# Two steps share one network of 512 tokens in float32r, with weights streamed from DRAM

## The chip, the cores and the metric

One core of one Trainium2 chip runs the kernel. The metric is device microseconds per execution. The engines are TensorE (PE, with its weight loads as PEld), VectorE (DVE), ScalarE (ACT), GpSimd (POOL) and SyncE (SP), which issues DMAs.

## The reference

A gated linear attention over 768 positions feeds a two-layer network with a PReLU between the layers.

```python
# q, k, v, f_logit: (4, 8, 768, 48);  w_in (384, 2048), w_out (2048, 384), alpha (2048,)
f = 1 / (1 + exp(-f_logit))
for t in range(768):
    state = f[:, :, t, :, None] * state + einsum('bhd,bhe->bhde', k[:, :, t], v[:, :, t])
    y[:, :, t] = einsum('bhd,bhde->bhe', q[:, :, t], state)
x = y.transpose(0, 2, 1, 3).reshape(3072, 384)
h = x @ w_in
out = (maximum(h, 0) + alpha * minimum(h, 0)) @ w_out
```

## The kernel before

The 3072 tokens are cut into 12 steps: step n = (c, bp) has 128 positions (C) of two batches (U), that is T = 256 tokens; c goes from 0 to 5, bp is 0 or 1, and n = 2c + bp. Each step has an attention part and a network part, and the network of step n runs beside the attention of step n+1.

The order of work on PE, DVE and ACT is written out by hand. Every part is a generator that is advanced piece by piece, and `ORDER` lists which generator comes next. The letters in it: `P` (prepare, six pieces), `O` (carry, one), `S` (attend, six), `n` (network, 13 pieces, or 12 for the first step), `a w b v` (the unpacking of the weights), `W` (sums of blocks of w_out). Steps 0 and 1 have a finer alphabet. The DMAs on SP and POOL are not in that list; they wait for what they need, in the order in which their queue has them. From step 4 on the order repeats (`USUAL`): "S n2 S n2 O n Q n3 Q S2 n Q S n Q S n Q n Q n", where Q is the prepare part of the step after.

The pieces that the prediction's steps speak of:
- `prepare` piece 1 calls `loaded` (lines 264 to 297): POOL loads f, q, k and v of the step (L272, L281), ACT takes the sigmoid (L283), and DVE makes running products of f. Piece 2 is two scans. Piece 3 (L336, L342) is the last to read f. Pieces 4 and 5 scale keys and queries; piece 5 transposes scaled keys on DVE into `kt` (L413). Piece 6 copies queries into A on ACT (L380) and issues sixteen small DMAs on SP from `kt` to `ksn` (L422). Each of f, q, k, us, ps and ksn has one buffer; y uses that of ksn.
- `carry` multiplies `ksn` by v (L436), takes the cross terms (L463) and moves the state (`moved`, L447 and L451, on DVE).
- `attend` has two pieces of scores (L489, L498) with masked copies on DVE (L506, L553), two pieces that place the blocks on ACT (L513), one that multiplies by v (L521), and one that moves the state, copies y and sends it by ten DMAs on three queues to xT (`by_token`, L533).
- `network`: eight pieces of the first layer, each for two feature tiles of 128 in one PSUM bank (12 records in the trace), then ACT (L721) and DVE (L723) make the gate, and after every fourth piece DVE makes four sums (L800). The second layer is a Strassen-Winograd form of seven products of eight matmuls of 192 columns (L755) with five `plus` on DVE (L759). Step 0 has the plain second layer instead (L736, 32 matmuls of 384 columns).

```python
kt = late["kt"].tile([128, W], F32, tag="kt", name=f"kt_{i}")
```

In the kernel before this tile has a buffer of its own. PSUM has four banks for the network (`bank`) and two pairs of banks for attention (`pair`).

Of the kernel before, what the change touches and what calls it, by code (L numbers as in the profile page):

```python
# [8 lines left out]
F32 = mybir.dt.float32  # L9
I16 = mybir.dt.int16  # L10
# [4 lines left out]
AF = mybir.ActivationFunctionType  # L15
# [6 lines left out]
U = 2  # L22
# [6 lines left out]
UP = 2.0 ** 16  # L29

# [5 lines left out]
        "n0 1u1 1u0 n0 1U0 b v 1U1 P2 1H0 1A0 v 1d n0 1H1 b 1t 1D v 1y0 1A1 1y1 v W 1Y0 P2 1Y1 W 1X W W n0 1M P2 P2 "  # L36
        "P2 n0 n1 S2 P2 W n1 n1 n1 n1 ",
        "S2 S2 P3 n1 P3 n1 n1 O2 P3 S2 n1 n1 S2 P3 P3 n1 S2 n1 n1 S3 n2 P3 n2 S3 n2 n2 P4 n2 S3 S3 n2 O3 n2 n2 S3 S3 "
        "P4 n2 P4 n2 P4 P4 n2 P4 n2 n2 ",
)  # L40
USUAL = "S n2 S n2 O n Q n3 Q S2 n Q S n Q S n Q n Q n"

def flat(head, usual, steps=12):
    out = []
    for word in " ".join(head).split():
        if word in "awbvW":
            out.append((word, None))
        elif word[0] in "01":
            out.append((word[1:], int(word[0])))
        else:  # L50
            out.append((word[0], int(word[1:])))
    for n in range(len(head), steps + 1):
        for key in usual.split():
            for _ in range(int(key[1:] or 1)):
                k = key[0]
                m = n - 1 if k == "n" else n + 1 if k == "Q" else n
                if 0 <= m < steps:
                    out.append(("P" if k == "Q" else k, m))
    return out

ORDER = flat(HEAD, USUAL)
# [3 lines left out]
def kernel(  # L65
# [57 lines left out]
    staging = ExitStack()  # L123
    stage = staging.enter_context(tc.tile_pool(name="stage", bufs=1))
# [10 lines left out]
    w_in_sb = const.tile([128, NK, DF], F32, tag="w_in", name="w_in_sb")  # L135
    w_out_sb = const.tile([128, NF, DM], F32, tag="w_out", name="w_out_sb")
    NH, DH = NF // 2, DM // 2
    gate = const.tile([128, NH, 2, T], F32, tag="gate", name="gate")
# [244 lines left out]
    def prepare(bp, c, x):  # L383
# [28 lines left out]
        kt = late["kt"].tile([128, W], F32, tag="kt", name=f"kt_{i}")  # L412
# [125 lines left out]
    def attend(bp, c, x):  # L538
# [32 lines left out]
        xT = x["T"] = work.tile([128, NK, T], F32, tag="xT", name=f"xT_{i}")  # L571
# [3 lines left out]
    def opening(bp, x):  # L575
# [110 lines left out]
        def given():  # L686
            xT = x["T"] = work.tile([128, NK, T], F32, tag="xT", name=f"xT_{i}")
            if bp:
                by_token(x["y"], xT)
            else:  # L690
                for kt in range(NK):
                    nc.scalar.copy(xT[:, kt], x["xt"][kt][:, 0:T])
# [13 lines left out]

    def network(bp, c, x):
        i = f"{bp}_{c}"
        xT = x["T"]
        plain = (bp, c) == steps[0]  # L710
        for f in range(NH):
            ph = bank(f"ph{f}_{i}")
            tiles = (2 * f, 2 * f + 1) if plain else (f, f + NH)
            for kt in range(NK):
                for j, m in enumerate(tiles):
                    nc.tensor.matmul(ph[:, j * T:(j + 1) * T], lhsT=w_in_sb[:, kt, m * 128:(m + 1) * 128],  # L716
                                     rhs=xT[:, kt], start=(kt == 0 and j == 0), stop=(kt == NK - 1 and j == 1),
                                     skip_group_check=True)
            neg = work.tile([128, 2, T], F32, tag="neg", name=f"neg{f}_{i}")
            phv = ph.rearrange("p (j t) -> p j t", j=2)  # L720
            nc.scalar.activation(neg, phv, AF.Relu, scale=-1.0)  # L721
            for j, m in enumerate(tiles):
                nc.vector.scalar_tensor_tensor(gate[:, m % NH, m // NH], neg[:, j], om[:, m:m + 1], phv[:, j],  # L723
                                               ALU.mult, ALU.add)
            if not plain and f % 4 == 3:
                sums(slice(f - 3, f + 1))
            yield

        def store(u, o):
            t0 = ((U * bp + u) * NC + c) * C  # L730
            nc.sync.dma_start(out=out[t0:t0 + C], in_=o)

        if plain:
            po = [bank(f"po{u}_{i}") for u in range(U)]
            for n, (f, u) in enumerate([(f, u) for f in range(NF) for u in range(U)]):
                nc.tensor.matmul(po[u][:, 0:DM], lhsT=gate[:, f % NH, f // NH, u * C:(u + 1) * C], rhs=w_out_sb[:, f],  # L736
                                 start=(f == 0), stop=(f == NF - 1))
                if n % 8 == 7 and n != U * NF - 1:
                    yield
            for u in range(U):  # L740
                o = work.tile([128, DM], F32, tag="o", name=f"o{u}_{i}")
                nc.scalar.activation(o, po[u][:, 0:DM], AF.Copy, scale=UP)
                store(u, o)
            yield
            return

        a11, a12, a22 = (lambda f, j=j, u=u: gate[:, f, j, u * C:(u + 1) * C] for j, u in ((0, 0), (1, 0), (1, 1)))
        s1, s2, s3, s4 = (lambda f, n=n: late["S"][:, n, f] for n in range(4))
        b11, t1, b21, b22 = (lambda f, r=r, d=d: w_out_sb[:, NH * r + f, DH * d:DH * (d + 1)]
                             for r, d in ((0, 0), (0, 1), (1, 0), (1, 1)))  # L750
        t2, t3, t4 = (lambda f, t=t: late[t][:, f] for t in ("t2", "t3", "t4"))

        def product(to, of, by, more=False):
            for f in range(NH):
                nc.tensor.matmul(to[:, 0:DH], lhsT=of(f), rhs=by(f), start=(f == 0 and not more), stop=(f == NH - 1),  # L755
                                 skip_group_check=True)

        def plus(to, of, by, scale=UP):
            nc.vector.scalar_tensor_tensor(to, of[:, 0:DH], scale, by, ALU.mult, ALU.add)  # L759

        o0, o1 = (work.tile([128, DM], F32, tag="o", name=f"o{u}_{i}") for u in range(U))
        kept, u2, u3 = (late["C"][:, n] for n in range(3))
        pa, pb = (bank(f"p{n}_{i}") for n in "ab")
        product(pa, a11, b11)
        product(pb, a22, t4)
        nc.scalar.activation(kept, pa[:, 0:DH], AF.Copy, scale=UP)
        yield
        pc, pd = (bank(f"p{n}_{i}") for n in "cd")
        product(pc, s2, t2)
        product(pd, s1, t1)  # L770
        plus(u2, pc, kept)
        yield
        product(pa, a12, b21, more=True)
        product(pc, s3, t3, more=True)
        plus(o0[:, DH:DM], pd, u2)
        nc.scalar.activation(o0[:, 0:DH], pa[:, 0:DH], AF.Copy, scale=UP)  # L776
        yield
        pe = bank(f"pe_{i}")
        product(pe, s4, b22)
        plus(u3, pc, kept)  # L780
        plus(o1[:, 0:DH], pb, u3, -UP)
        plus(o1[:, DH:DM], pd, u3)
        store(1, o1)
        yield
        plus(o0[:, DH:DM], pe, o0[:, DH:DM])
        store(0, o0)
        yield

    late = {}

    def sums(fs_):

        s = late["S"]
        u0, u1 = slice(0, C), slice(C, T)
        of = lambda j, u: gate[:, fs_, j, u]
        for to, x_, y_, op in ((s[:, 0, fs_], of(0, u1), of(1, u1), ALU.add),
                               (s[:, 1, fs_], s[:, 0, fs_], of(0, u0), ALU.subtract),
                               (s[:, 2, fs_], of(0, u0), of(0, u1), ALU.subtract),
                               (s[:, 3, fs_], of(1, u0), s[:, 1, fs_], ALU.subtract)):
            nc.vector.tensor_tensor(to, x_, y_, op)  # L800

    def halves_of_w_out():

        staging.close()
        pool = ctx.enter_context(tc.tile_pool(name="late", bufs=1))
        late["kt"] = pool
        late["S"] = pool.tile([128, 4, NH, C], F32, tag="S", name="S")
        late["C"] = pool.tile([128, 3, DH], F32, tag="C", name="Csum")
        for n in ("t2", "t3", "t4"):
            late[n] = pool.tile([128, NH, DH], F32, tag=n, name=n)  # L810
        yield
        b11, b12, b21, b22 = (w_out_sb[:, NH * r:NH * (r + 1), DH * d:DH * (d + 1)] for r in range(2) for d in range(2))
        t2, t3, t4 = (late[n] for n in ("t2", "t3", "t4"))

        for to, x_, y_, op in ((t3, b22, b12, ALU.subtract), (t2, t3, b11, ALU.add), (t4, t2, b21, ALU.subtract),
                               (b12, b12, b11, ALU.subtract)):
# [3 lines left out]
            yield  # L820
# [8 lines left out]
    pieces["W"] = halves_of_w_out()  # L829

    with tc.manual_schedule(engines={mybir.EngineType.PE, mybir.EngineType.DVE, mybir.EngineType.Activation}):
# [3 lines left out]
        for n, (bp, c) in enumerate(steps):  # L835
            x = {}
            run["n", n] = network(bp, c, x)
# [6 lines left out]
        for key, n in ORDER:  # L844
            part = pieces[key] if n is None else run[key, n]
            part() if callable(part) else next(part)

# [54 lines left out]
```

## Time and profile before

| | |
|---|---|
| time, median of 3 runs (lowest to highest) | 606.79 us (604.29 to 607.48) |
| span of the profiled execution, first to last instruction | 604.5 us |
| DVE busy | 495.7 us (82%) |
| ACT busy | 249.5 us (41%) |
| granted TensorE clock | 1.00 throughout |
| DMA moved | 50.41 MB, 83 GB/s on average |
| length of a step from step 3 on | 46.7 to 48.9 us |

The profile is of one execution; no time of its own is given beside its span, and the three runs are other executions. Shares of busy time are averages over the whole span; the stretches in the table of busy time show one step each.

### The profile page before, as it was taken

How to read it: one execution, taken by the hardware profiler on the slowest of the kernel's cores; microseconds unless marked ns; L12 is line 12 of the kernel's file. 1: busy time of each engine (PE TensorE's matmuls, PEld its weight loads, DVE VectorE, ACT ScalarE, POOL GpSimd, SP SyncE). 2: the span in 40 equal slices, each digit the busy share in tenths (PEclk: the TensorE clock that was granted, in tenths of full speed). 3: DMA queues.
4: the chain of work that ended last, by engine and by line, in shares of the span. 5: the costliest groups of instructions: out<-in, count | busy, mean ns of one | idle time of the engine just before them, and what ended most of it. 6: DMA issues, size and time to landing. Idle time of an engine off the chain costs nothing.

```text
span 604.5 us, 18724 instructions
## 1 busy us (share of the span) xinstructions
PE 585.7 (97%) x8040; PEld 526.9 (87%) x8040; DVE 495.7 (82%) x997; ACT 249.5 (41%) x478; POOL 62.8 (10%) x117
## 2 busy tenths in 40 slices
PE   5689999999999999999999999999999999999997
PEld 5678768898898899899899899799899899889997
DVE  7799999998898888889889899798798798761351
ACT  5988943712622442452452361262161363232110
POOL 8210010010010010010020020001001000000000
PEclk9999999999999999999999999999999999999999
DMA  8969132324232242232233223303314401201000
GB/s 284 359 209 381 38 88 50 76 62 104 49 88 31 81 101 38 58 104 46 61 87 63 65 54 94 66 37 97 81 36 89 90 3 30 52 2 28 27 1 27
DMA packets 68115, 50.41 MB, mean 83 GB/s; under 512 B 47168, under 2 KB 60608, under 8 KB 68032
## 3 DMA queue, kind: packets, MB, share of 16 engines
q1 hardware_dynamic: 56656, 25.01, 15.6%
q0 software_dynamic: 6864, 22.35, 13.1%
q10 hardware_dynamic: 4512, 1.85, 1.6%
q8 instruction: 64, 1.05, 0.8%
q14 instruction: 19, 0.16, 0.1%
HBM read 36.21 MB, written 4.72 MB: 68 GB/s over the span
## 4 chain that ended last, share of the span: by engine, by line
PE 90%; DVE 4%; ACT 2%; DMA 2%; SPq 1%; issue 1%; DVEq 0%; ACTq 0%
PE ph L716 40%; PE pc L755 9%; PE pa L755 9%; PE pb L755 5%; PE pe L755 4%; PE pd L755 4%; PE py L521 4%; PE po L736 4%; PE qu L498 3%; PE raw L489 3%; PE pd L436 2%; PE off L463 1%; SPq L422 1%; DMA ksn<-kt 1%; DMA f<-in_fT 1%
## 5 line engine op out<-in xcount | busy, mean ns | idle before, releaser
L716 PE MATMUL ph<-xT,w_in_sb 128*128 128x256 f32 x1152 | 257.6, 382 | 0.9 <-issue 0.9
L716 PEld LDWEIGHTS ph<-xT,w_in_sb 128*128 128x128 f32 x1152 | 216.2, 190 | 33.3 <-issue 3.1
L721 ACT ACTIVATE neg<-ph 128x512 f32<-128x512 f32 x96 | 57.0, 596 | 175.2 <-PE ph L716 136.6
L723 DVE SCALAR_TENSOR_TENSOR gate<-neg,om,ph 128x256 f32<-128x256 f32 x192 | 82.5, 477 | 41.3 <-ACT neg L721 41.1
L755 PE MATMUL pc<-t,S 128*128 128x192 f32 x352 | 61.6, 328 | 0.0
L755 PE MATMUL pa<-w_out_sb,gate 128*128 128x192 f32 x352 | 61.1, 327 | 0.0
L755 PEld LDWEIGHTS pa<-w_out_sb,gate 128*128 128x128 f32 x352 | 57.9, 190 | 0.6
L755 PEld LDWEIGHTS pc<-t,S 128*128 128x128 f32 x352 | 57.4, 190 | 0.5
L553 DVE COPY_PREDICATED ad<-mquad,qu 128x224 f32<-128x224 int32 (+6 forms) x140 | 41.9, 299 | 6.2
L506 DVE COPY_PREDICATED ad<-mraw,raw 128x256 f32<-128x256 int32 (+1 forms) x96 | 42.2, 442 | 3.2 <-PE raw L489 0.5
L380 ACT COPY A<-q 48x512 f32<-48x512 f32 x44 | 27.1, 617 | 35.5 <-DVE q L354 35.1
L513 ACT COPY A<-ad 32x256 f32<-32x256 f32 x96 | 38.8, 404 | 1.5
L776 ACT ACTIVATE o<-pa 128x192 f32<-128x192 f32 x11 | 3.6, 330 | 84.2 <-PE pa L755 77.3
L397 DVE TENSOR_TENSOR us<-us,fs 128x768 f32<-128x768 f32 (+5 forms) x60 | 36.6, 611 | 0.1
L759 DVE SCALAR_TENSOR_TENSOR Csum<-pc,Csum 128x192 f32<-128x192 f32 x22 | 7.9, 357 | 29.7 <-PE pc L755 29.3
L800 DVE TENSOR_TENSOR S<-gate 128x512 f32<-128x512 f32 x44 | 30.3, 688 | 0.8
L755 PE MATMUL pb<-t,gate 128*128 128x192 f32 x176 | 30.4, 326 | 0.0
L755 PE MATMUL pe<-w_out_sb,S 128*128 128x192 f32 x176 | 30.4, 326 | 0.0
L755 PE MATMUL pd<-w_out_sb,S 128*128 128x192 f32 x176 | 30.4, 326 | 0.0
L325 ACT COPY us<-qd 128x256 f32<-128x256 f32 x48 | 27.0, 672 | 7.4 <-DVE qd L289 4.4
L289 DVE TENSOR_TENSOR qd<-qd,f 128x768 f32<-128x768 f32 (+2 forms) x36 | 27.1, 752 | 3.2 <-ACT qd L285 3.2
L498 PE MATMUL qu<-us,k 48*32 48x112 f32 (+1 forms) x1536 | 26.1, 259 | 3.8 <-ACT ad L633 2.2
(114 smaller groups left out, 743.6 us busy)
## 6 DMA issues: line engine op xcount, KB each, us to landing
w_out_raw<-in_w_out SPq DMA_DIRECT2D x8, 767.8 KB, 8.4
w_in_raw<-in_w_in SPq DMA_DIRECT2D x8, 767.2 KB, 13.0
q<-in_qT POOLq DMA_DIRECT2D x11, 512.0 KB, 4.2
f<-in_fT POOLq DMA_DIRECT2D x11, 512.0 KB, 4.3
k<-in_kT POOLq DMA_DIRECT2D x11, 512.0 KB, 4.7
out<-o SPq DMA_DIRECT2D x24, 192.0 KB, 2.3
vs<-in_v POOLq DMA_DIRECT2D x22, 192.0 KB, 4.7
ksn<-kt SPq DMA_DIRECT2D x80, 32.0 KB, 2.0
```

The source lines that it names most:

```text
L289: nc.vector.tensor_tensor(qdv[d], qdv[d - 1][:, :, :, 1:5 - d], f[:, :, 1:5 - d].rearrange("p (g i) r -> p g i r", i=NB), ALU.mult)
L380: nc.scalar.copy(A[halves(cc)[1], :, par * HP:(par + 1) * HP, CH * cc:CH * (cc + 1)], x["q3"][rows(par)].rearrange("p (u h c) s t -> p u h ...
L397: nc.vector.tensor_tensor(by_four(us[:, :, UO[m]:UO[m] + 4 * n]), by_four(us[:, :, skip:skip + 4 * n]), spread(fq[:, :, 1:1 + n], n), ALU. ...
L498: nc.tensor.matmul(qu[DB * j:DB * (j + 1), par, hp * QS + 4:hp * QS + QL], lhsT=x["k4"][r_, g * DB:(g + 1) * DB], rhs=x["us"][r_, g, 4:QL] ...
L506: nc.vector.copy_predicated(adu[:, :, :, d:4], mraw[:, d, :, d:4].bitcast(I32).unsqueeze(1).broadcast_to((128, H, NB, n)), rv[:, :, QO[d]: ...
L513: nc.scalar.copy(A[s_, u, :, s_], ad[s_, u].rearrange("p r h t -> p (r h) t"))
L553: nc.vector.copy_predicated(ad[:, u, :, :, 4 * m:DB], mquad[:, lo:lo + n].bitcast(I32).unsqueeze(1).unsqueeze(1).broadcast_to((128, 2, HP, ...
L716: nc.tensor.matmul(ph[:, j * T:(j + 1) * T], lhsT=w_in_sb[:, kt, m * 128:(m + 1) * 128], rhs=xT[:, kt], start=(kt == 0 and j == 0), stop=( ...
L721: nc.scalar.activation(neg, phv, AF.Relu, scale=-1.0)
L723: nc.vector.scalar_tensor_tensor(gate[:, m % NH, m // NH], neg[:, j], om[:, m:m + 1], phv[:, j], ALU.mult, ALU.add)
L755: nc.tensor.matmul(to[:, 0:DH], lhsT=of(f), rhs=by(f), start=(f == 0 and not more), stop=(f == NH - 1), skip_group_check=True)
L800: nc.vector.tensor_tensor(to, x_, y_, op)
```

## The change

From step 4 on, the two steps of one c share a network of 512 tokens (`joint`), as pieces `N`; the first four networks stay single and all have the plain second layer, in 17 pieces.

The first layer of `joint` uses float32r operands. x is split in xh (rounded), xl = x - xh and xs = xl + EPS xh (`split_of_x`, pieces `X`); w_in is split likewise once, into three parts per feature tile (`split_of_w_in`, pieces `Z` in steps 2 to 5), which SP writes to DRAM in sixteen DMAs. Per feature tile there are nine matmuls of 512 columns: six into a bank, an ACT pass that scales the bank in place, and three more into it one piece later (`last`).

The second layer is again seven products, now with the features of the step bp = 0 and the step bp = 1 as the two halves of rows, each over two groups of 128 tokens, in float32. Its blocks and sums of w_out are written to DRAM (`W`, now in step 6).

All weights of `joint` are read from DRAM through a ring of 6 buffers of 590 KB (later 11): 16 units of w_in and 10 of w_out per pair. A unit is asked for on SP when the matmuls that used its buffer are done.

The parts of a core's memory are rearranged for this: the weights' tiles and the single gate are given back at `T`, and `kt` uses the buffer of `f`. The repeating order becomes one for even and one for odd steps, and the last pair's network stands alone at the end.

```diff
+EPS = 2.0 ** -12
+ROUND = 1.0 + 2.0 ** -13
+FIRST = 4
+RING = 6, 5
 HEAD = (
...
-        "n0 1u1 1u0 n0 1U0 b v 1U1 P2 1H0 1A0 v 1d n0 1H1 b 1t 1D v 1y0 1A1 1y1 v W 1Y0 P2 1Y1 W 1X W W n0 1M P2 P2 "
-        "P2 n0 n1 S2 P2 W n1 n1 n1 n1 ",
-        "S2 S2 P3 n1 P3 n1 n1 O2 P3 S2 n1 n1 S2 P3 P3 n1 S2 n1 n1 S3 n2 P3 n2 S3 n2 n2 P4 n2 S3 S3 n2 O3 n2 n2 S3 S3 "
-        "P4 n2 P4 n2 P4 P4 n2 P4 n2 n2 ",
+        "n0 1u1 1u0 n0 n0 1U0 b v 1U1 P2 1H0 1A0 v 1d n0 n0 1H1 b 1t 1D v 1y0 1A1 1y1 v V 1Y0 P2 1Y1 1X n0 n0 1M P2 "
+        "P2 P2 n0 n0 n0 n1 S2 P2 n1 n1 n1 n1 ",
+        "n1 S2 n1 n1 O2 n1 P3 n1 n1 P3 S2 S2 Z n1 P3 S2 n1 P3 S2 n1 P3 n1 P3 n1 n1 ",
+        "S3 n2 S3 n2 n2 O3 n2 P4 n2 n2 Z P4 S3 S3 n2 P4 Z S3 n2 P4 S3 n2 P4 Z n2 P4 n2 ",
+        "S4 n2 S4 n2 n2 O4 n2 P5 n2 Z P5 S4 S4 n2 n3 P5 Z S4 n3 P5 S4 n3 P5 Z n3 P5 n3 ",
+        "S5 n3 S5 n3 O5 n3 P6 n3 P6 Z S5 S5 n3 P6 S5 n3 P6 S5 n3 n3 P6 n3 P6 n3 n3 T X2 X2 n3 ",
 )
-USUAL = "S n2 S n2 O n Q n3 Q S2 n Q S n Q S n Q n Q n"
+EVEN = "S N2 S N2 O N2 Q N2 Q S2 N2 Q S N2 Q S N2 Q N Q N"
+ODD = "S N S N O N Q N2 Q S2 N2 Q S N Q S N2 Q N Q X N2 X N2"
+LAST = "N16 N15"
...
-        kt = late["kt"].tile([128, W], F32, tag="kt", name=f"kt_{i}")
+        kt = work.tile([128, W], F32, tag="f", name=f"kt_{i}", bufs=1)
...
+            while self.free and self.asked < self.known:
+                n = self.asked % UNITS
+                at = self.held[self.asked] = self.free.pop(0)
+                if n < NF:
+                    nc.sync.dma_start(out=at.bitcast(F32), in_=parts_of_w_in[:, n])
...
+    def split_of_x(c):
...
+            nc.scalar.activation(xh[:, :, s_], xT[:, :, s_], AF.Copy, scale=ROUND)
+            nc.vector.tensor_tensor(xl[:, :, s_], xT[:, :, s_], xh[:, :, s_].bitcast(F32), ALU.subtract)
+            nc.vector.scalar_tensor_tensor(xs[:, :, s_], xh[:, :, s_].bitcast(F32), EPS - 1.0, xT[:, :, s_],
+                                           ALU.mult, ALU.add)
...
+    def split_of_w_in():
...
+            nc.scalar.activation(at[:, 0], w, AF.Copy, scale=-EPS * ROUND)
+            for k in (1, 2):
+                nc.vector.scalar_tensor_tensor(at[:, k], at[:, 0].bitcast(F32), 1.0 / EPS + 1.0 - k, w, ALU.mult, ALU.add)
+            for j in range(2):
+                nc.sync.dma_start(out=parts_of_w_in[:, 2 * f + j].rearrange("p (x n) -> p x n", n=128),
...
+    def joint(c):
...
+        def passes(m, parts, start):
+            u = ring.held[base + m].rearrange("p (s a n) -> p s a n", s=3, a=NK)
+            for n, (s_, by) in enumerate(parts):
+                for kt in range(NK):
+                    nc.tensor.matmul(banks[m], lhsT=u[:, s_, kt], rhs=by[:, kt], start=start and n + kt == 0,
+                                     stop=not start and kt == NK - 1, skip_group_check=True)
...
+        def last(m):
+            passes(m, ((2, xs),), False)
+            ring.done(base + m)
+            ph = banks.pop(m).rearrange("p (r t) -> p r t", r=2)
+            to = g[:, m // NH, :, m % NH]
+            nc.scalar.activation(to, ph, AF.Relu, scale=-1.0)
+            nc.vector.scalar_tensor_tensor(to, to, om[:, m:m + 1], ph, ALU.mult, ALU.add)
+            if m in (3, 7):
+                minus(slice(m - 3, m + 1))
...
+        for m in range(NF):
+            banks[m] = bank(f"ph{m}_{i}")
+            passes(m, ((0, xh), (1, xl)), True)
+            nc.scalar.activation(banks[m], banks[m], AF.Copy, scale=EPS - 1.0)
+            if m:
+                last(m - 1)
+            yield
...
+        def product(to, block, half, start=True):
+            for f in range(4 * half, 4 * half + 4):
+                r = next(row)
+                n, k = base + NF + r // ROWS, r % ROWS
+                by = ring.held[n][:, k * DH:(k + 1) * DH].bitcast(F32)
+                for t in range(U):
+                    nc.tensor.matmul(to[:, t * DH:(t + 1) * DH], lhsT=block[:, f, t * C:(t + 1) * C], rhs=by,
...
```

`minus` subtracts four tiles of one step's gate from the other's, and `sum_` forms a sum or difference over eight tiles in two instructions of 1024 columns.

## The prediction

> **What bounds the kernel now.** I read the page first: the busy shares, then the chain of work that ended last.
>
> ```profile
> PE 585.7 (97%) x8040; PEld 526.9 (87%) x8040; DVE 495.7 (82%) x997; ACT 249.5 (41%) x478; POOL 62.8 (10%) x117
> PE 90%; DVE 4%; ACT 2%; DMA 2%; SPq 1%; issue 1%; DVEq 0%; ACTq 0%
> ```
>
> TensorE (PE) is the bound: 97% busy and 90% of the chain. VectorE (DVE) has 82%, so little room. Then the table of busy time by stretch, cut where attention step 5, step 11 and the last network begin:
>
> ```profile
> 233.09:279.77 46.68, 46.68 (x664) 42.69 (x671) 41.30 (x86) 17.88 (x36) 4.46 (x7) 1.00 0.31 69
> 515.58:562.24 46.66, 46.66 (x657) 42.89 (x658) 23.79 (x55) 11.06 (x25) 1.07 (x2) 1.00 0.13 28
> 562.24:604.50 42.26, 38.92 (x209) 36.15 (x207) 14.47 (x31) 5.44 (x10) 0.00 (x0) 1.00 0.04 15
> ```
>
> Columns: stretch, length, busy PE, weight load, DVE, ACT, POOL, granted clock, DMA share, GB/s. A middle step is 46.7 us, all PE, with 41.3 of DVE beside it. The end is one network alone, 42.3 us. The groups by form price PE:
>
> ```profile
> L716 PE MATMUL ph<-xT,w_in_sb 128*128 128x256 f32 x1152 | 257.6, 382 | 0.9 <-issue 0.9
> L736 PE MATMUL po<-w_out_sb,gate 128*128 128x384 f32 x64 | 21.4, 491 | 0.0
> ```
>
> 1152 records are 12 steps x 48 matmuls x 2: a float32 matmul is two records. The chain has 96 of them in 20.72 us (215.8 ns each), 16 of 192 columns in 2.60 (162.5 ns), 32 of 384 in 10.52 (329 ns).
>
> Last, because the diff puts `kt` into the buffer of `f`, the timelines of VectorE, SyncE, TensorE, ScalarE and GpSimd from one transpose to the next:
>
> ```profile
> 264.83 1.20 DVE L336 TENSOR_TENSOR us<-us,f 128x1024 f32<-128x1024 f32 x1
> 266.33 0.72 POOL L272 DMA_DIRECT2D f<-in_fT  x1 [10.32 <-DVE us L336]
> 276.90 1.25 DVE L413 STREAM_TRANSPOSE kt<-ks 128x1024 f32<-128x1024 f32 x1
> 278.22 2.58 SPq L422 DMA_DIRECT2D ksn<-kt  x4
> 281.72 9.11 SPq L422 DMA_DIRECT2D ksn<-kt  x12
> 293.95 0.94 PE L436 MATMUL pd<-vs,ksn 64*48 64x48 f32 x64
> 299.07 1.06 ACT L283 ACTIVATE f<-f 128x1024 f32<-128x1024 f32 x1
> 323.68 1.25 DVE L413 STREAM_TRANSPOSE kt<-ks 128x1024 f32<-128x1024 f32 x1
> ```
>
> `f` for the next step is fetched as soon as L336 has read the old one (264.8), 33 us before the sigmoid (299.1). `kt` is ready at 278.15; sixteen DMAs need SP until 290.8, land 2.0 us later (292.8), and L436 starts at 293.95.
>
> **PE's work.** The first layer of steps 4 to 11 is now 8 x 48 x 2 records x 215.8 = 165.7 us. It becomes 4 pairs x 16 tiles x 9 = 576 float32r matmuls of 512 columns, which the trace does not have. Bounds: the row of 256 columns doubled, two records, 863 ns (as float32, +331 us); a quarter of it, one pass, 215.8 ns, 124.3 us, a gain of 41.4. I take the quarter: the change cuts every operand to a rounded head and an exact rest so that no partial product is left over, which is pointless unless one pass is all that is done. The weight load (190 ns) hides beside 215.8 as it does now beside 162.5. The Trainium skill, FP8 and Floating Point Precision (TensorE Precision Notes), has true FP32 in four passes and a reduced FP32 that is truncated on reading; by it the quarter holds too, and no run here shows it.
>
> The second layer of a pair is 56 rows x 2 x 2 records = 224 x 162.5 = 36.4 us, as two networks now. Networks 1 to 3 lose their seven-product form: 64 x 329 = 21.1 against 112 x 162.5 = 18.2, so +2.9 each, +8.6. Sum for PE: -41.4 + 8.6 = -32.8. Were PE still the bound throughout, the span would be 571.7.
>
> **DVE's work.** Of the 41.3 us of a step, L723 has 6.9, L800 5.2, L759 2.0; attention is 27.3. In a pair, sixteen L723-like operations of 512 columns cost some 0.70 (0.43 now, plus 256 columns at the 0.27 that 512 cost over 256 in TENSOR_TENSOR): 11.2; `minus` and `sum_` are eight of 1024 columns at 1.14 (9.1); six `plus` of 384 at 0.55 (3.3); the split of x four of 768 at 0.9 (3.6). So 27 us a pair where there were 28: nothing won. The even step of a pair (first layer) has PE 31.1 + 7.1 of attention = 38.2 against 41 of DVE; the odd one PE 43.5 against 41. `split_of_w_in` adds 16 of 768 columns (15 us) in steps 2 to 5, where the sums that go (3 x 5.2) pay for it. `halves_of_w_out` moves into step 6 (7.1).
>
> **The new wait.** `kt` and `f` share one buffer (bufs=1). So the next `f` can be loaded only when all sixteen ksn DMAs have read `kt`; what was prefetched 33 us ahead joins a loop: kt -> ksn 14.7 us (278.15 to 292.8) -> f 4.7 (median landing of the f load in the two steps around it) -> sigmoid 1.1 -> DVE's chain to the next transpose. That chain is, of the 25.9 us from 299.07 to 324.93, 14.1 us of prepare's own instructions; the rest is what the written order puts between. The wait stands on POOL, with q, k and v loads behind it, and then on ACT at the sigmoid, with the evacuations of the network behind that. Before, the same sum would have been 14.7 + 4.7 + 25.9 = 45.3, just inside 46.7: room of 1.4 us, had the buffer been shared then. After:
> - Odd step: 14.7 + 4.7 + 1.1 + 14.1 + three `sum_` 6.9 + `plus` 1.1 + `moved` 2.1 = 44.7; with ring reads on the same queue and engines, 46.
> - Even step: from kt on, DVE has the rest of prepare 2.0, x 3.6, `plus` 2.7, lags and quads 8.3, `moved` 2.1, gates 4.2 = 23, longer than ksn and f (19.4); then 1.1 + 14.1 + eight gates 5.6 + `minus` 1.1 + `moved` 2.1 = 24: 47.
> - Steps 3, 4, 5: 19.4 + 15.2 + 2.1 + gates 3.5, 2.6, 0 + w_in's parts 3.7, 3.7, 1.9 = 43.9, 43.0, 38.6, and about 1 each for handing over.
>
> PE has no part in these, so what it saves there turns into idle time before L436 and behind DVE.
>
> **Ring and DRAM.** A unit is 128 x 1152 x 4 bytes, 590 KB, one per 9 matmuls (1.94 us): 304 GB/s while the first layer runs unmixed, about 225 when mixed. Slices of the page show 359 and 381 GB/s, so eleven slots suffice and I cost steady reads at nothing, covered by units asked some 15 us ahead; bare, it is up to 0.5 us a unit. In step 6 there is no cover: the first reads stand behind sixteen ksn DMAs on SP (12.4 us) and need 4 to land, and 5.5 MB of w_out rows go out meanwhile. First matmul at kt + 13 (10 if read early, 16 if not); six tiles, two scored halves and carry 16.8; then 24 of DVE plus two W sums 3.6: 58 us.
>
> **Sum.** The transpose for step 3 ends at 138 (now 135.1): n0 still ends at 91.5, then eight first-layer pieces 21.1, scores 3.6, carry 1.6, sigmoid and DVE 19 or so, as P3 now stands behind O2. Steps 3 to 5: 266. Step 6: 324. Steps 7 to 10: 46 + 47 + 46 + 47: 510. Step 11: 14.7 to carry, 1.6, 2.0 of outputs, twelve half products 31.2: 559.5. The last pair alone 31.1 + 36.4: 627. Tail as now, 3.4: a span of 630. Around the profiled 604.5 us lies 2.3 to the median of the runs, 606.8: 633 us.
>
> **Rivals.**
> 1. *The shared buffer does not decide* (f's load comes early enough, or its loop overlaps more than I see). Then DVE and PE carry the steps at 43 to 45: transposes at 256 for step 6, 306, and 482 for step 11, and the same end of 120: 602 + 2 = 604. For: ksn and f are 1.4 us from harmless in the sum above. Against: the order is fixed and every term is a row.
> 2. *PE stays the bound*, the other side: DVE's lag in even steps is made up in odd ones, banks and transfers hide. It decides once transposes follow each other in under 42 us. Span 571.7, with half of the 18 us by which DVE's work exceeds PE's in steps 3, 4 and 6 (40 to 36, 38 to 34, 48 to 38): 581 + 2 = 583. For: from 41 to 91 us both engines stand above 97%. Against: kt -> ksn -> f alone leaves 22.6 us of 42 to a DVE chain of 25.
> 3. *SP blocks*: ring reads wait for PE ahead of ksn in one queue; each such wait lengthens the loop, some 4 us in eight steps: 630 + 32 + 2 = 664.
> 4. *A float32r pass runs at half rate* (431.7 ns): even steps 69 us instead of 47, last pair +31: 630 + 66 + 31 = 727 + 2.
> 5. *The change doesn't do what it says*: float32r at float32's price would be beyond 900; hardly.
>
> **How the numbers follow.** Chances: forecast 0.58, rival 1 0.10, rival 2 0.11, rival 3 0.16, rival 4 and 5 0.05. Within 0.5% (3 us, about what a measurement of this kernel can tell from no change) lies half of rival 1: 0.05; faster takes rival 2 and a fifth of rival 1: 0.13; slower the rest, 0.82. Range: down to 598, which leaves out rival 2; up to 668, which takes in rival 3 and leaves out rival 4. The forecast's own spread is 615 to 645 (each step +-1.5, step 6 +-5).
>
> **What would show it.** Right: the f load on POOL waits for ksn DMAs, its landing is followed within 1 us by the sigmoid; transposes 45 to 48 us apart in steps 7 to 10; PE under 90%, idle ahead of L436 and of the gates; float32r records about 216 ns apart; the last pair 67 us. Wrong: transposes under 43 us apart, or f landing long before the sigmoid (rivals 1, 2); SP waiting for matmuls in the middle of ksn (3); records of 430 ns (4).

## The result and the profile after

The changed kernel takes 693.5 us (median of 4 runs, 692.96 to 696.42) against 607.1 for the kernel before: 1.145 times as long, 95% interval 1.141 to 1.148. The forecast was 633 with a range to 668: the sign was right, the size was not. Each run below has its median time and its ratio to the kernel before, measured beside it, with a 95% interval; executions that were disturbed (one of ksn on two queues took 1955 us) are left out.

The page first, with the busy shares, the granted clock in 40 slices and the chain of work that ended last:

```profile
PE 594.4 (86%) x7704; PEld 490.8 (71%) x7704; DVE 492.9 (71%) x871; ACT 297.8 (43%) x550; POOL 63.0 (9%) x117
PEclk9999999999999898999989889989989998999999
PE 49%; DVE 20%; ACT 12%; DMA 8%; SPq 6%; issue 4%; ACTq 0%; DVEq 0%; POOLq 0%
```

PE went from 90% of the chain to 49%: nothing bounds the kernel throughout any more. PE's busy time did not fall by 32.8 us, it rose by 8.7. The groups of the first layer show why that figure misleads:

```profile
L874 PE MATMUL ph_p<-xs,ring 128*128 128x512 f32 x192 | 58.9, 416 | 10.6 <-ACT ph_p L893 10.6
L874 PE MATMUL ph_p<-xh,ring 128*128 128x512 f32 x192 | 57.2, 406 | 2.8 <-DVE gate L886 2.8
L874 PE MATMUL ph_p<-xl,ring 128*128 128x512 f32 x192 | 55.5, 398 | 1.0 <-DVE xl L802 1.0
```

A record lasts some 400 ns, though unbroken ones follow each other every 226 (below): where waits break a run of them each record counts for longer, and so the 576 records are "busy" for 171.6 us. The table of busy time by stretch says where (same columns as before; the first line is of the kernel before, up to the transpose that opens step 7, the others of the kernel after):

```profile
0.00:324.93 324.93, 310.74 (x4544) 275.13 (x4545) 291.75 (x569) 159.04 (x300) 46.54 (x91) 1.00 0.40 113
```

```profile
0.00:335.30 335.30, 289.94 (x4179) 220.75 (x4184) 274.51 (x506) 173.85 (x319) 45.95 (x90) 0.96 0.62 184
335.30:390.50 55.20, 43.94 (x612) 40.50 (x605) 38.03 (x68) 15.61 (x30) 4.47 (x7) 0.94 0.70 208
390.50:453.90 63.40, 50.40 (x669) 40.81 (x674) 45.66 (x80) 30.28 (x56) 4.47 (x7) 0.92 0.70 208
565.60:617.90 52.30, 48.54 (x679) 45.96 (x678) 27.44 (x49) 12.29 (x25) 1.07 (x2) 0.93 0.53 145
617.90:650.50 32.60, 32.60 (x144) 26.52 (x143) 13.48 (x17) 17.71 (x30) 0.00 (x0) 1.00 0.89 291
650.50:688.30 37.80, 37.08 (x227) 36.65 (x226) 12.39 (x15) 2.18 (x4) 0.00 (x0) 1.00 0.07 25
```

Up to step 7 PE has 21 us less work (289.9 for 310.7), and yet the step starts 10 us later. Steps 7 and 8 are 55.2 and 63.4 us long (46.8 and 47.8 before), with PE and DVE both under 80%, a clock of 0.92 to 0.94 and the DMA engines 70% busy. The last pair alone is 32.6 + 37.8 us.

Ends of the transposes into `kt` (VectorE's timeline), which cut the time into the steps of the prediction:

| stretch, us | before | forecast | after |
|---|---|---|---|
| start to step 3 | 135.1 | 138 | 142.0 |
| steps 3, 4, 5 | 143.1 | 128 | 135.8 |
| step 6 | 46.8 | 58 | 57.5 |
| steps 7 to 10 | 186.8 | 186 | 230.3 |
| step 11 to the end of the span | 92.8 | 120 | 126.1 |

So 44 of the 62 us by which the span (691.7) passes the forecast one (630) lie in steps 7 to 10: 12 in the odd ones (55.1 and 48.5 us, forecast 46 each), 33 in the even ones (63.5 and 63.2, forecast 47 each). Two views show what these steps wait for. The odd step 7, from the timelines of DVE, SyncE, GpSimd and ScalarE:

```profile
326.15 2.54 ACTq L550 DMA_DIRECT2D xT<-y  x4
334.09 1.25 DVE L430 STREAM_TRANSPOSE kt<-ks 128x1024 f32<-128x1024 f32 x1
334.23 3.26 SPq L550 DMA_DIRECT2D xT<-y  x4
337.58 2.83 SPq L787 DMA_DIRECT2D ring<-rows_of_w_out  x3
343.24 11.83 SPq L439 DMA_DIRECT2D ksn<-kt  x16
357.12 0.73 POOL L289 DMA_DIRECT2D f<-in_fT  x1 [12.24 <-DMA ksn<-kt]
364.01 1.06 ACT L300 ACTIVATE f<-f 128x1024 f32<-128x1024 f32 x1 [4.65 <-DMA f<-in_fT]
```

`kt` is ready at 335.3, but SP starts its sixteen ksn DMAs 8 us later; `f` is asked for at 357.1 and lands 6.9 us later, where the forecast had 4.7. From transpose to sigmoid it takes 28.7 us (the forecast: 14.7 + 4.7). What ksn waits for is in the waits of SyncE (engine and line, what it waited for, us in total, times, longest) and in the DMA view of 330 to 345 us (traffic of the stretch; an issue's count, size and median us to landing):

```profile
SPq L439 <- DMA xT<-y: 2.6, 2, 2.4
```

```profile
DMA packets 1902, 5.68 MB, mean 379 GB/s; under 512 B 272, under 2 KB 723, under 8 KB 1900
xT<-y SPq DMA_DIRECT2D x3, 48.0 KB, 7.3
```

`y` shares the buffer of ksn, so ksn may be written only when the ten xT DMAs have read `y`. Two things make these late. ScalarE issues its four at 326.2, as soon as `y` is copied, but SyncE issues its four only at 334.2: ring reads stand ahead of them in its order, and between 318 and 335 us it waits there for DMAs (6.3 us for the rows of w_out that step 6 writes to DRAM, 3.5 for earlier ring reads). And once issued, three of SyncE's four need 7.3 us (median) to land, while the ring's reads move 379 GB/s on average. This is so in step 7 alone: in steps 8 to 11 SyncE starts ksn within 0.1 us of the transpose.

The even step 8, from the timelines of PE, ScalarE and DVE, and two stretches of the table:

```profile
397.73 8.26 PE L906 MATMUL pe_p<-ring,gate 128*128 128x192 f32 x32 [9.64 <-DVE o_p L912]
391.87 2.50 ACT L397 COPY A<-q 48x512 f32<-48x512 f32 x4 [12.46 <-DVE q L371]
394.38 1.58 ACT L801 ACTIVATE xh<-xT 128x768 fp32r<-128x768 f32 x2
395.25 0.96 DVE L802 TENSOR_TENSOR xl<-xT,xh 128x768 fp32r<-128x768 f32 x1 [2.68 <-ACT xh L801]
397.11 0.56 DVE L912 SCALAR_TENSOR_TENSOR o_p<-pe_p,sums 128x384 f32<-128x384 f32 x1
388.00:397.70 9.70, 0.09 (x1) 0.00 (x0) 6.88 (x15) 4.04 (x6) 0.00 (x0) 0.77 0.20 24
397.70:406.00 8.30, 8.28 (x40) 8.05 (x48) 3.10 (x5) 0.00 (x0) 0.73 (x1) 0.65 0.57 121
```

PE may add to `pe_p` only after `plus(right(o1), pe, v)` (L912) has read its first half. That `plus` stands on DVE behind the rest of prepare and the split of x, and the split waits for ScalarE, which first copies into A. PE stands for 9.6 us, and the 32 records that follow (16 matmuls, two records each) run at a clock of 0.65: 8.3 us, where 32 such records take 5.4 us elsewhere in this trace. That a pause lowers the clock for the work behind it is what the Trainium skill has in TensorE: Matmul & The Clock Gate (Part 1: The HAM clock gate). The forecast's sum has no term for it.

### The profile page after: what moved, and what is told of

It is laid out like the page before. It is cut to its first block, busy times and chain, and to the rows that moved or that the text cites. A ratio compares the mean times of both kernels' runs of the same rounds, so it can differ in the third digit from the quotient of the medians.

```text
span 691.7 us, 18229 instructions
## 1 busy us (share of the span) xinstructions
PE 594.4 (86%) x7704; PEld 490.8 (71%) x7704; DVE 492.9 (71%) x871; ACT 297.8 (43%) x550; POOL 63.0 (9%) x117
## 4 chain that ended last, share of the span: by engine, by line
PE 49%; DVE 20%; ACT 12%; DMA 8%; SPq 6%; issue 4%; ACTq 0%; DVEq 0%; POOLq 0%
PE ph_p L874 12%; PE ph L740 8%; PE po L751 5%; PE pe_p L906 5%; SPq L439 5%; PE pa_p L906 4%; DMA f<-in_fT 3%; ACT A L530 3%; PE py L538 3%; DMA xT<-y 3%; PE pc_p L906 2%; PE qu L515 2%; DVE us L414 2%; ACT A L397 2%; DVE ad L570 2%
## 5 line engine op out<-in xcount | busy, mean ns | idle before, releaser
L740 PE MATMUL ph<-xT,w_in_sb 128*128 128x256 f32 x384 | 90.0, 393 | 0.0
L751 PE MATMUL po<-w_out_sb,gate 128*128 128x384 f32 x256 | 86.8, 496 | 0.0
L740 PEld LDWEIGHTS ph<-xT,w_in_sb 128*128 128x128 f32 x384 | 74.4, 197 | 12.2 <-issue 1.2
L886 DVE SCALAR_TENSOR_TENSOR gate<-gate,om,ph_p 128x512 f32<-128x512 f32 x64 | 47.2, 746 | 44.8 <-ACT gate L885 44.3
L751 PEld LDWEIGHTS po<-w_out_sb,gate 128*128 128x128 f32 x256 | 48.7, 193 | 32.8 <-issue 1.9
L874 PE MATMUL ph_p<-xs,ring 128*128 128x512 f32 x192 | 58.9, 416 | 10.6 <-ACT ph_p L893 10.6
L906 PE MATMUL pe_p<-ring,gate 128*128 128x192 f32 x256 | 47.4, 348 | 18.6 <-DVE o_p L912 18.6
L874 PE MATMUL ph_p<-xh,ring 128*128 128x512 f32 x192 | 57.2, 406 | 2.8 <-DVE gate L886 2.8
L874 PE MATMUL ph_p<-xl,ring 128*128 128x512 f32 x192 | 55.5, 398 | 1.0 <-DVE xl L802 1.0
L906 PE MATMUL pa_p<-ring,gate 128*128 128x192 f32 x256 | 46.5, 338 | 0.0
L906 PEld LDWEIGHTS pa_p<-ring,gate 128*128 128x128 f32 x256 | 44.5, 199 | 0.9
L515 PEld LDWEIGHTS qu<-us,k 48*32 48x32 f32 x1536 | 23.5, 117 | 28.7 <-issue 15.5
```

Source lines behind the costliest of these rows:

```text
L515: nc.tensor.matmul(qu[DB * j:DB * (j + 1), par, hp * QS + 4:hp * QS + QL], lhsT=x["k4"][r_, g * DB:(g + 1) * DB], rhs=x["us"][r_, g, 4:QL] ...
L874: nc.tensor.matmul(banks[m], lhsT=u[:, s_, kt], rhs=by[:, kt], start=start and n + kt == 0, stop=not start and kt == NK - 1, skip_group_ch ...
L886: nc.vector.scalar_tensor_tensor(to, to, om[:, m:m + 1], ph, ALU.mult, ALU.add)
L906: nc.tensor.matmul(to[:, t * DH:(t + 1) * DH], lhsT=block[:, f, t * C:(t + 1) * C], rhs=by, start=start and f + t == 0, stop=f == NH - 1 a ...
```

## The experiments

Four theories were on the table: the shared buffer of `kt` and `f` (the forecast's own), the order around `plus`, the ring's reads (their bytes, or their place on SP's queue), and ScalarE's extra pass; later, whether an engine's work bounds the steps after all.

**The loop by itself.** In the kernel before, `kt` goes into f's buffer and nothing else changes.

```diff
-        kt = late["kt"].tile([128, W], F32, tag="kt", name=f"kt_{i}")
+        kt = work.tile([128, W], F32, tag="f", name=f"kt_{i}", bufs=1)
```

> The kernel before with only kt put into the buffer of f. Theory (ksn 14.7, f load 4.7 and 25.9 to the next transpose are 45.3 of a step of 46.7): 0 to 1.5 us a step from step 3 to 10, 607 to 616 us. Rival (the shared buffer alone is what made the change slow): over 630 us.

Measured 613.7, ratio 1.011 (1.009 to 1.013). The timelines of DVE, SyncE, GpSimd and ScalarE of one step:

```profile
285.20 1.25 DVE L413 STREAM_TRANSPOSE kt<-ks 128x1024 f32<-128x1024 f32 x1
290.02 9.07 SPq L422 DMA_DIRECT2D ksn<-kt  x12
301.73 0.73 POOL L272 DMA_DIRECT2D f<-in_fT  x1 [24.37 <-DMA out<-o]
307.46 1.06 ACT L283 ACTIVATE f<-f 128x1024 f32<-128x1024 f32 x1
```

`f` is now issued 15 to 16 us behind the transpose, when ksn is through, and no longer 35 (the bracket names another DMA as the last of GpSimd's waits; ksn, issued until 299.1, lands some 2 us later). Yet transposes stay 46.7 to 47.7 us apart in steps 4 to 9, and step 10 has 44.5 as before. Step 3 alone grew, from 48.2 to 55.8: there ksn starts 6.4 us behind the transpose, in the kernel before too, and the sigmoid moves from 19.0 to 26.6 us behind it. The forecast's "room of 1.4 us" in this loop was right for the usual steps.

**Control, and kt back in a buffer of its own.** Room for it is made with rings of 5 and 5 units and four raw buffers; the control has only these.

```diff
-RAWS, LEADS = 5, 4
+RAWS, LEADS = 4, 4
...
-RING = 6, 5
+RING = 5, 5
...
-        kt = work.tile([128, W], F32, tag="f", name=f"kt_{i}", bufs=1)
+        kt = work.tile([128, W], F32, tag="kt", name=f"kt_{i}", bufs=1)
```

> The changed kernel with one buffer less for unpacking the weights (RAWS 4) and one less in the ring (RING 5, 5), which makes room for the next kernel's own buffer: its control. Theory (ring reads are far enough ahead): 693 +-3 us. Rival (the ring is the limit, its reads land late): a slot in eleven is lost, over 705 us.

> The control with kt in a buffer of its own, so that f is prefetched as before the change. Theory (the f load behind ksn sets the sigmoid in steps 4, 5, 7 and 9): 1.7 to 6.6 us each come back, 12 to 18 us in all, 675 to 681 us, and the sigmoid never waits for the f load. Rival (the loop is ksn, carry and the scores; f hides behind them): within 4 us of the control.

Control: 696.0, ratio 1.147 (1.140 to 1.155), the same as the kernel after within the intervals: a unit less does no measurable harm. Own buffer: 685.9, ratio 1.130 (1.124 to 1.136). It gives 10 us back, fewer than expected. Odd steps fall to 50.0 and 46.4 (53.0 and 49.3 in the control), even ones stay at 63, and PE still waits 6.6 us for `plus` in each.

**plus ahead of the split of x.** One place in the written order of the odd steps, on the kernel after:

```diff
-ODD = "S N S N O N Q N2 Q S2 N2 Q S N Q S N2 Q N Q X N2 X N2"
+ODD = "S N S N O N Q N2 Q S2 N2 Q S N Q S N2 Q N2 Q X N X N2"
```

> The changed kernel with one piece N of the odd steps moved ahead of the last piece of prepare and of the split of x, so that the plus that reads pe stands on DVE ahead of the split. Theory (in odd steps PE waits some 9.6 us for this plus, then runs about 3 us at a lower clock): steps 8 and 10 get 8 to 13 us shorter each, 667 to 677 us, granted clock in them from 0.92 to 0.97 or more. Rival (even steps are bound by the transfers or by ACT's scaling of the bank): 690 us or more, the wait moves to another place.

Measured 682.5, ratio 1.124 (1.122 to 1.127): 11 us less, again fewer than expected. PE's timeline at the same place in steps 8 and 10:

```profile
394.37 7.95 PE L906 MATMUL pe_p<-ring,gate 128*128 128x192 f32 x32 [5.04 <-DVE o_p L912]
500.28 5.47 PE L906 MATMUL pe_p<-ring,gate 128*128 128x192 f32 x32 [3.83 <-DVE o_p L912]
```

The waits were 9.64 and 9.00, and the matmuls 8.26 and 6.92: 9.8 us less waiting and 1.8 less at a low clock. The two steps shortened by 5.6 and 6.8 us; the granted clock in them went from 0.92 to 0.94 and 0.97.

**Both edits together**, with the control's rings.

> Both edits of the first call: kt in its own buffer (with RAWS 4 and RING 5, 5) and the piece with the plus moved ahead. Theory (the two act on different steps, odd and even, and add up): 696 - 10 - 11 = 675 us, 672 to 678. If one only uncovers the other: 680 us or more.

Measured 671.9, ratio 1.108 (1.104 to 1.112): 24 under the control, where the two alone give 21, within the intervals. They are separate waits, one in odd and one in even steps. Steps 7 to 10 take 207.6 us (230.3).

**The ring's reads.** Once with a ninth of the bytes of each read (128 of 1152 columns; the weights used are not those of the reference, and the second part of the ring is set to zero first), once with all of them issued on GpSimd instead of SP:

```diff
-                    nc.sync.dma_start(out=at.bitcast(F32), in_=parts_of_w_in[:, n])
+                    nc.sync.dma_start(out=at[:, 0:128].bitcast(F32), in_=parts_of_w_in[:, n, 0:128])
```

```diff
-                    nc.sync.dma_start(out=at.bitcast(F32), in_=parts_of_w_in[:, n])
+                    nc.gpsimd.dma_start(out=at.bitcast(F32), in_=parts_of_w_in[:, n])
```

(and in each the same for `rows_of_w_out`).

> The changed kernel in which each of the 104 ring reads moves a ninth of its unit, 128 elements a row instead of 1152 (the other weights in the ring are stale or zero); the DMAs, their order and their waits are the same. Theory A (the bytes hardly matter, order and waits do; only the f load and ksn land 2 us sooner in odd steps): 682 to 690 us. Rival B (the bytes on the 16 engines slow ksn, f and xT): steps 7 to 10 lose 5 us or more each, below 672 us.

> The changed kernel with the ring reads issued by GpSimd instead of SP. Theory A (on SP a ring read that waits for PE holds up ksn, 8 us in step 7, little elsewhere): step 7 gets 5 to 8 us shorter, 683 to 690 us, unless the reads on GpSimd now hold up the f, q and k loads. Rival B (every step is held up by ring reads ahead of ksn and xT on SP): below 675 us. Rival C (the waits move to the loads on GpSimd): 693 us or more.

Short reads: 680.1, ratio 1.123 (1.117 to 1.129), 13 us less, between the ranges of theory A and rival B. On GpSimd: 694.65, ratio 1.146 (1.144 to 1.148), no change, in the range of rival C (what moved to GpSimd, though, is the wait ahead of xT, as shown below). Step 7 with short reads, on SyncE, GpSimd and ScalarE:

```profile
336.82 11.33 SPq L439 DMA_DIRECT2D ksn<-kt  x16
352.99 0.73 POOL L289 DMA_DIRECT2D f<-in_fT  x1 [6.18 <-DVE vs L464]
357.17 1.06 ACT L300 ACTIVATE f<-f 128x1024 f32<-128x1024 f32 x1
```

and in the DMA view of 330 to 345 us:

```profile
DMA packets 3481, 0.68 MB, mean 45 GB/s; under 512 B 2715, under 2 KB 3477, under 8 KB 3478
xT<-y SPq DMA_DIRECT2D x1, 48.0 KB, 2.1
```

`kt` was ready at 336.8, and SP starts ksn at once: its xT DMAs were issued at 327.6, together with ScalarE's, and are through in 2.1 us. `f` lands 4.0 us after its issue (6.9). So the reads cost step 7 the 8 us ahead of ksn and 3 us of `f`, and the step falls from 55.2 to 46.8; steps 8 to 10 get 2 to 3 us shorter each. With the reads on GpSimd, SyncE issues its xT at once too, but two of the ten xT DMAs are GpSimd's, and now these stand behind ring reads (`y` is copied at 331.7):

```profile
336.78 0.56 POOL L550 DMA_DIRECT2D xT<-y  x1
338.37 0.56 POOL L550 DMA_DIRECT2D xT<-y  x1 [1.03 <-DMA ring<-parts_of_w_in]
339.65 1.25 DVE L430 STREAM_TRANSPOSE kt<-ks 128x1024 f32<-128x1024 f32 x1
348.51 12.25 SPq L439 DMA_DIRECT2D ksn<-kt  x16
```

They take 10.7 us (median) to land, and SyncE starts ksn 7.6 us after the transpose. This edit moved the place in the queue from SyncE to GpSimd, so it does not tell that place from the traffic; the short reads took both away at once. No run here has the full reads on a queue that no xT DMA uses.

**ScalarE's scaling pass** left out (the banks are then not scaled between the passes):

```diff
-            nc.scalar.activation(banks[m], banks[m], AF.Copy, scale=EPS - 1.0)
```

> The changed kernel without ACT's pass that scales each bank in place (the first layer's sums are then combined without the factor). Theory A (PE waits for that pass where ACT has 3 to 5 us of attention copies ahead of it, some 4 to 6 us in each even step, and some of it returns through DVE): even steps 63 to 57 or 59 us, 677 to 684 us. Theory B (PE's waits before the last pass are hidden elsewhere): over 690 us. If ACT as a whole set the even steps, 64 passes of 0.58 would give 37 us: 656 us.

Measured 688.3, ratio 1.136 (1.132 to 1.141): 5 us less, between theory A and the 690 of theory B. The even steps are 2.4 and 3.7 us shorter, the odd ones 2.9 and 1.4. In the profiled execution (691.5 us, the longest of the four) step 7 opens 8.8 us later than in the kernel after, before most of these passes run, so the gain in steps 7 to 10, 10 us there, is larger than the 5 us of the whole time.

**Constant work for PE in the pause**, to hold the clock up: 24 matmuls on `ones` ahead of the second half of `pe`.

```diff
         plus(right(o1), pe, v)
         product(pd, a22, 1)
         yield
+        filler = bank(f"fill_{i}")
+        for _ in range(24):
+            nc.tensor.matmul(filler[:, 0:DH], lhsT=ones[:, 0:128], rhs=ones[:, 0:DH], start=True, stop=True)
```

> The changed kernel with 24 matmuls of constants on PE where it waits for the plus that reads pe (they write a bank that nobody reads). They take 7.8 us at full clock where PE stood idle 9.6. Theory (the idle time itself lowers the clock for the matmuls behind it: 32 records took 8.3 us instead of 5.2): the granted clock in the 8 us behind the wait rises from 0.65 to 1.0, steps 8 and 10 lose 2 to 3 us each, 685 to 690 us. Rival (the clock falls for another reason, or costs nothing there): 692 us or more.

Measured 712.9, ratio 1.174 (1.171 to 1.177): slower. PE's timeline:

```profile
389.35 7.96 PE L966 MATMUL fill_p<-ones 128*128 128x192 f32 x48
399.15 5.47 PE L906 MATMUL pe_p<-ring,gate 128*128 128x192 f32 x32 [1.84 <-DVE o_p L912]
421.05 0.32 PE L480 MATMUL off<-q,kh 48*32 48x32 f32 x5 [3.00 <-issue]
```

The 32 records take 5.5 us again, at a granted clock of 1.00, so the clock was the pause's doing. But the filler runs in every pair, also in the last two, where there is no pause, 8.0 us each time: the time from step 11 on grows from 126.1 to 142.3. And where it fills a pause the step gains little: step 8 is 66.0 us (63.5), with a new pause of 3.0 us later on (the last line), step 10 61.3 (63.2).

**More around ksn and x**, on the kernel with both edits: ksn on two queues, the split of x earlier, and both.

```diff
-                nc.sync.dma_start(
+                (nc.sync if (4 * a + b) % 2 else nc.gpsimd).dma_start(
...
-ODD = "S N S N O N Q N2 Q S2 N2 Q S N Q S N2 Q N2 Q X N X N2"
+ODD = "S N S N O N X Q N2 Q S2 N2 Q S N Q S N2 Q N2 X Q N N2"
```

> The version with both edits (672 us), and the sixteen ksn DMAs issued in turn by GpSimd and SP instead of SP alone. Theory (without the shared buffer the loop is still transpose, ksn, carry, and then the next prepare behind carry in the written order; ksn is 12 us of issue in it): the transposes of steps 3 to 5, 7 and 9 come 3 to 6 us closer each, 648 to 660 us. Rival (these steps are bound by DVE's work or by ACT): 668 us or more.

> The version with both edits (672 us), with the first half of x split right after carry of the odd step and the second half ahead of prepare's last piece, so ahead of ACT's 2.5 us of copies. Theory (in even steps the first matmul of the pair waits some 9 us after the transpose for copies and split): 3 to 5 us each in steps 8, 10 and at the last pair, 660 to 666 us. Rival (PE's own work and the pauses at ACT carry the even steps): 669 us or more.

> All edits together: kt in its own buffer, plus and split of x moved ahead, ksn on two queues. Theory (they act on different steps): 672 - 18 - 9 = 645 us, 636 to 655. If the bound below them is DVE's work or the transfers: 658 us or more. In every case above the kernel before (607 us), since the last pair's network alone takes 70 us behind the last attention step.

Measured 668.5 (ratio 1.102, 1.098 to 1.106), 677.7 (1.116, 1.112 to 1.121) and 671.5 (1.107, 1.104 to 1.110): the theories missed all three times, and all three lie in the ranges of the rivals. Two queues gained 3 us of the 12 or more expected, within the intervals. With x split earlier, ScalarE waits for x itself, as the list of waits has it (engine and line, what it waited for, total, times, longest):

```profile
ACT xh L801 <- DMA xT<-y: 13.0, 2, 6.8
```

**Is an engine the bound after all?** On the kernel with both edits: one pass less for PE, and, apart from it, no `minus` and no `sum_` for DVE.

```diff
-            passes(m, ((0, xh), (1, xl)), True)
+            passes(m, ((0, xh),), True)
...
-            if m in (3, 7):
-                minus(slice(m - 3, m + 1))
...
-        sum_(a22, a22, a21, ALU.add)
...
-        sum_(a11, a11, a22, ALU.add)
...
-        sum_(a12, a12, a22, ALU.subtract)
```

> The kernel with kt in a buffer of its own and plus ahead of the split of x (671.9 us) with the middle pass of the first layer left out: per feature tile six float32r matmuls instead of nine, so the output lacks the product of w_in's parts with xl. PE loses 3 x 16 x 232 ns = 11.1 us in each of the four pairs. Theory A (in the three pairs beside attention the time goes round through ksn, DVE, ACT and PE in the written order, and PE is not the bound): only the last pair and the tail give it back, and perhaps 1 to 3 us of each even step: 651 to 661. Rival B (PE with its first layer sets the even steps after all): four times 11: 626 to 632.

> The same kernel (671.9 us) without minus and without the three sum_, so the output is formed from unsummed gates: DVE loses about 9 us in each of four pairs. Theory A (waits for hand-overs set the steps, no engine's work): 1 to 3 us a pair where DVE stands in the chain: 660 to 668. Rival B (VectorE's work sets the steps): three pairs of 9 and some of the last: 640 to 647.

Measured 663.5 (ratio 1.098, 1.091 to 1.104) and 669.2 (1.103, 1.099 to 1.108). Busy time of steps 7 to 10 and, in the first two, from step 11 to the end, in the kernel with both edits, with a pass less, and without the sums:

```profile
336.83:544.42 207.59, 182.41 (x2494) 158.20 (x2482) 164.61 (x286) 90.83 (x172) 15.18 (x24) 0.96 0.70 211
544.42:671.10 126.68, 118.43 (x1045) 109.51 (x1044) 53.14 (x81) 32.14 (x59) 1.07 (x2) 0.97 0.49 151
```

```profile
339.31:543.72 204.41, 168.98 (x2431) 146.88 (x2431) 164.14 (x286) 90.59 (x172) 15.18 (x24) 0.90 0.69 214
543.72:658.50 114.78, 106.53 (x998) 99.25 (x997) 52.94 (x81) 32.14 (x59) 1.07 (x2) 0.99 0.51 168
```

```profile
333.05:537.65 204.60, 181.58 (x2530) 158.56 (x2529) 146.86 (x270) 90.83 (x172) 15.19 (x24) 0.96 0.72 216
```

With a pass less PE is busy 13.4 us less in steps 7 to 10, and they shorten by 3.2; behind step 11 it is busy 11.9 less, and 11.9 come back in full. Without the sums DVE is busy 17.8 us less there, and the steps again shorten by 3.0. So neither engine's work alone sets these steps. Two things qualify this. With a pass less the granted clock fell from 0.96 to 0.90 in these steps, which takes back part of the work that was saved. And without the sums the odd steps are 3.8 and 8.0 us shorter (45.7 and 38.7), the even ones 4.3 and 4.4 longer (60.8 and 59.3): DVE's sums do count in the odd steps, and the even step behind gives it back. Both works taken out at once was not run. Both times came out 1 to 3 us above the range of theory A and 20 or more from the rivals.

**The found causes put together:** both edits, no scaling pass and short reads.

> The same kernel (671.9 us) with the scaling pass of ScalarE left out and each ring read a ninth of its bytes (the weights used are then not those of the reference). Alone, on the kernel after, these were worth 5 and 13 us. Theory A (the losses are separate waits, as kt's buffer and plus turned out to be): 651 to 657. Rival B (they are the same waits that the two edits already removed): 662 to 669.

Measured 661.7, ratio 1.089 (1.085 to 1.094): 10 us less, not 18, at the near edge of rival B. Part of what the reads and the scaling cost was the same wait that the two edits had taken away: with both edits ksn still starts 6.5 us late in step 7, but the step is 49.5 us, as `f` no longer stands behind ksn, and here it is 46.6. The profiled execution (656.3 us, the shortest of the four) has steps 7 to 10 at 197.4 us and 124.9 behind them.

**ksn on two queues in the kernel before** (the first hunk of the diff further up), the one edit that these runs suggest for it (its carry waited for ksn in some steps):

> The kernel before (about 606.5 us) with the sixteen ksn DMAs on GpSimd and SyncE in turn instead of all on SyncE. Theory A (PE is the bound and ksn ready 1.2 us ahead of the carry in most steps): no change, 605 to 608. Rival B (the wait for ksn at 411 to 435 us is paid on the path): 601 to 604, faster than either kernel.

Measured 603.74 (10 runs) against 606.27 (13), ratio 0.997 (0.996 to 0.999): rival B, and the fastest of all these kernels, though by less than 0.5%. The last ksn DMAs and the carry in one step, on SyncE and PE, before and with two queues:

```profile
424.11 10.31 SPq L422 DMA_DIRECT2D ksn<-kt  x12
435.88 0.26 PE L436 MATMUL pd<-vs,ksn 64*48 64x48 f32 x2 [0.37 <-DMA ksn<-kt]
```

```profile
424.68 1.89 SPq L422 DMA_DIRECT2D ksn<-kt  x3
435.47 0.71 PE L436 MATMUL pd<-vs,ksn 64*48 64x48 f32 x44
```

The issue is over at 426.6 instead of 434.4, and the carry finds ksn there. Two steps that were 47.8 us are 47.0 and 46.6. (The profiled execution took 605.5 us, one of the longer of the ten.)

## Why the prediction was right and wrong

- **PE's price for float32r: right.** 144 matmuls of the last pair take 32.6 us, 226 ns each (the quarter price was 215.8). The last pair is 70.4 us against the forecast 67.5; rivals 4 and 5 fell with it.
- **"What it saves there turns into idle time": right.** PE has 21 us less before step 7 and none of it shows. What the pairing puts off, two steps' networks behind the last attention step instead of one, is paid in full: 126.1 us from step 11 on, 120 forecast, 92.8 before; the excess is 2.9 in the last pair and 2.8 in step 11 (52.3, forecast 49.5). The run with a pass less shows both halves: PE work counts at the end and not in the steps.
- **Step 6: right** (57.5, forecast 58), as a sum, with some luck: the first float32r matmul comes 9.7 us behind the transpose, where 13 was forecast, and what follows takes longer. The terms were not tested one by one.
- **The forecast for the start and steps 3 to 5: 12 us short.** In the experiments on the kernel after, step 6 opens between 275 and 285 us, whatever the edit, and the cause stays open; from 234.0 to 277.8 PE is busy 34.6 of 43.8 us, at a clock of 0.82.
- **The odd step, "14.7 + 4.7 + 1.1 + 14.1 + ... 46": the loop was right, two terms were mis-sized, 12 of the 44 us.** From `kt` to the sigmoid step 7 has 28.7 us for 19.4: ksn starts 8 us late and `f` takes 6.9; in step 9 ksn is on time, `f` again takes 6.9, and the step is 48.5. The step that failed is "I cost steady reads at nothing". Eleven units cover PE's needs, and a unit less does no harm; what the reads delay is the attention's own transfers: y to xT, and through the buffer that y shares with ksn the ksn DMAs, then f. With short reads 13 us came back. Rival 3 put 4 us in each of eight steps on SP, with ring reads that wait for PE ahead of ksn. SP did stand behind ring reads in step 7, ahead of xT, but waiting for DMAs; the sixteen ksn issues then run unbroken. How much of the 8 us is that place in the queue and how much the longer landing stays open.
- **The even step, "24: 47": wrong, 33 of the 44 us, and the main step that failed.** The sum had DVE's work and the ksn loop, and no wait of PE for DVE. In the order that the diff prints, `plus(right(o1), pe, v)` has the split of x and prepare ahead of it, and the next matmuls into `pe` cannot start without it: 9.6 and 9.0 us of waiting, and 2.9 and 1.6 more at a low clock behind it. With `plus` moved, 11 us came back. The ScalarE pass, which the sum did not have, adds 5 to the whole time. With both edits the even steps still take 56.5 and 54.9 us, 8 to 10 over the forecast, about half of it behind the sigmoid (28.6 and 27.7 us for 24).
- **The shared buffer: right in kind, not the main term.** 10 us of 86, and 6 in the kernel before; the forecast hung the odd steps and steps 3 to 5 on it.
- **Not explained:** without all four causes steps 7 to 10 still take 197 us in the shortest execution, where the sum has 186 and the kernel before 187. With both edits alone, taking out either engine's work moves them by 3 us, so hand-overs between the engines are the likely place of these 10 us or more; no run here shows it. The four edits together bring 32 of the 60 us between 633 and 693.5.

## What to carry to other kernels

When a bound engine is relieved, cost the new steps as chains in the written order, not as loads: for each bank or buffer that is written again, ask which instruction must have read it, and what stands ahead of that instruction on its engine. Work that is put off to pair it up is paid in full at the end, where nothing hides it, while what was saved earlier may vanish. A stream of large reads is not free because its own buffers suffice: add what it does to the small transfers that share its queue and the DMA engines.

## What the runs showed of the hardware

The clock after a pause of PE was harder to foresee than expected. Ahead of the same 32 records (5.36 us where PE does not pause), pauses of 1.7 to 1.8 us left them at 5.5 us in the five places seen, pauses of 9.64, 9.00 and 5.04 made them 8.26, 6.92 and 7.95; between 2.1 and 3.8 us both occur, even for the same length: 2.84 us gave 5.47 in one kernel and 7.15 in another. By the Trainium skill, TensorE: Matmul & The Clock Gate (Part 1: The HAM clock gate), the clock halves after an idle window of about 3.4 us that runs freely. A free-running window fits the scatter, but here a pause of 2.09 us, behind 6.5 us of unbroken work at a clock of 1.00, was enough: the records behind it took 7.15 us, and the granted clock over 7.3 us was 0.77 (the kernel with both edits, step 8).

A large stream of reads slows other transfers beside it. In step 7 three xT DMAs of 48 KB took 7.3 us (median) to land and an `f` load of 512 KB 6.9; with short reads it was 2.1 and 4.0.
